# Linear attention beside a mixer MLP, one core: the last tile's queries move ahead of the products with wo, and those products are stacked

## The chip, the core and the metric

The kernel runs on one core of a Trainium2 chip. Five engines work side by side and tell one another by semaphores when data is ready: TensorE (PE in the profile) multiplies, VectorE (DVE) and ScalarE (ACT) do element-wise work, GpSimd (POOL) does the rest of it, and SyncE (SP) issues most DMAs. The metric is the device time of one execution in microseconds, the median of three runs.

## The reference

One sequence of 2048 tokens with 576 features goes through two blocks, and a gate per token mixes the two results:

```
q, k, v = split(x @ wqkv)                  # 32 heads of 18
phi = lambda t: where(t > 0, t + 1, exp(t)) + 1e-6
kv  = einsum("bhsd,bhse->bhde", phi(k), v)   # 18 x 18 per head
z   = sum over tokens of phi(k)
o   = (phi(q) . kv) / (phi(q) . z + 1e-6)
a   = o @ wo
b   = gelu(layernorm(x) @ w1 + b1) @ w2 + b2   # 576 -> 4608 -> 576
out = g * a + (1 - g) * b,   g = sigmoid(sum(x * gate_w))
```

## The kernel before

All products run on rounded operands (`fp32r`): each matrix is split into a high part, rounded, and a low part, the rounding error; a product is the sum of high x high, high x low and low x high. The 576 features are four slices of 128 and a tail of 64, whose high and low parts share one slice. So a projection of 128 tokens on 288 columns (half of 576) takes 14 matmuls: four HH, four HL, four LH and two TAIL, and `BY_ROWS` is the order HH and HL in turn (eight), then TAIL (two), then LH (four).

Every engine keeps program order: the order in which the code calls the operations is the order on each engine, up to the MLP, whose order a planner writes out. All operations go through one helper, so each row of the profile names line 125; they are told apart by their tiles. The stages are:

1. Start. Twelve matmuls on `ones` (`WARM`), then `first_keys` projects the first two tiles of tokens on the first half of the key weights (KEY, 0), with single matmuls on `ones` between the first ones (`warm`) and the transposes of the gate weights (`turn_gate`, into `column`). The second half of the key weights has two columns more, the gate weights and ones, for sums over x; they are written into the raw tile, which is then split as a whole.
2. For each of the 16 tiles of 128 tokens: keys, `phi`, products of x with `phi(k)` summed over all tokens (`add_products`), sums of the keys on GpSimd (`pks`), queries into `acc`. The last three tiles' queries (`late`) are left for stage 3. `jobs` hang other work into this loop by `at(step, ...)`.
3. The kv products: per group of seven heads (`GW` = 126 columns, five groups, the last one shifted so that it is 126 wide too) `wv` times the summed products gives `kv`; `mask_kv` keeps the blocks of one head each. The product of `kv` with `wo` is wanted in slices of 128 rows, so a slice takes pieces of two groups: nine `PIECES`, each with three terms and two halves, 54 matmuls (`project_values`). Each slice's result is taken over by ScalarE (high) and VectorE (low) into `wp`, in two pairs of banks in turn (`w_pairs`).
4. For each tile i: `weigh(i)` (GpSimd, queries times the sums z, into one of three places `qz`), `normalize(i)` (VectorE: reduce, two small operations, the queries in `acc` times the reciprocal), `tail_q(i)`, `transpose_q(i)` (five transposes on TensorE; copies to `qt` on ScalarE, low parts and tail of `qt` on VectorE) and `attend(i)`: 28 matmuls of `qt` with `wp`, per half in the order `BY_ROWS`.
5. The MLP as seven products in place of eight (Strassen), planned ahead, with the mixing at the end. It follows stage 4 and is not touched.

VectorE's two steps for `qt` stand at the end of `transpose_q`, with `q = qt[i]`:

```
dve.tensor_sub(q[:, 5:9], p, raw(q[:, 0:4]))
dve.scalar_tensor_tensor(q[:, 4], raw(q[:, 4]), low_half[:, 0:1], pe_, op0=OP.mult, op1=OP.add)
```

Of the kernel before, what the change touches and what calls it, by code (L numbers as in the profile page):

```python
# [17 lines left out]
P = 128  # L18
S, D, H, DH, F = 2048, 576, 32, 18, 4608
NT = S // P  # L20
# [15 lines left out]
EPS_LN = 1e-5  # L36
WARM = 12
FIRST = 3
# [56 lines left out]
def raw(ap):  # L95
    return ap.bitcast(F32)
# [35 lines left out]
def tile_gated_mix(ctx: ExitStack, tc: tile.TileContext, x, xm, xe, wm, we, wvm, wve, wo, um, ue, w2, b1, b2, gw, out):  # L132
# [95 lines left out]
    def load_w(part, half, pieces=((0, 5),), by=sp):  # L228
        if (part, half) not in wraw:
            wraw[part, half] = wsp.tile([P, 5, HALF + 2], F32, name="s", tag="s")  # L230
        s = wraw[part, half]
        main = wm[part * 2 + half].rearrange("p (t n) -> p t n", t=4)
        tail = we[part * 2 + half]
        for t0, t1 in pieces:
            if t0 < 4:
                by.dma_start(s[:, t0:min(t1, 4), :HALF], main[:, t0:min(t1, 4)])
            if t1 == 5:
                load_twice(s[:, 4, :HALF], tail, by)

    def split_w(part, half, by=dve, pieces=((0, 5),)):  # L240
        w = W[part, half]
        s = wraw[part, half][:, :, :w.shape[2]]
# [46 lines left out]

    def project(i, part, half, order=BY_ROWS, n=None, between={}):  # L290
        w = W[part, half]
        p = banks[i, part, half] = ps[:, next(halves_in) if n is None else n]
        for m, (a, b) in enumerate(order):
            pe.matmul(p[:, :w.shape[2]], xs[i][:, a, :], w[:, b], start=(m == 0), stop=(m == len(order) - 1))
            if m in between:
                between[m]()
# [174 lines left out]


    first = ORDER[:FIRST]
    gwr = spare[0:1, :5 * P]
# [5 lines left out]
    load_x(first[1], True)  # L480
    load_w(KEY, 1)
    load_x(first[2])
# [11 lines left out]
    split_w(KEY, 0, pieces=((0, 1), (1, 2), (2, 4)))  # L494
    split_tail(first[0])
    split_w(KEY, 0, pieces=((4, 5),))

    def first_keys(n, half, between={}):
        project(first[n], KEY, half, WEIGHTS_FIRST if n else HI_FIRST, 3 * half + n, between)
# [19 lines left out]

    first_keys(0, 0, {0: lambda: warm(1), 1: lambda: warm(1), 2: lambda: warm(1), 3: turn_gate})  # L520
    split_x(first[1])
    split_tail(first[1])
    first_keys(1, 0)
    dve.tensor_copy(wraw[KEY, 1][:, :, HALF:HALF + 1], column[:, :, None])
    dve.memset(wraw[KEY, 1][:, :, HALF + 1:HALF + 2], 1.0)
    split_w(KEY, 1, pieces=((0, 2), (2, 4), (4, 5)))
# [45 lines left out]

    PIECES = [(t, j) for t in range(5) for j in (t, t + 1) if j < G]
    kvs = wop_.tile([GW, len(PIECES), P], F32, name="kvs")
    pool.memset(kvs, 0.0)
    ysc = ExitStack()
    ysp = ysc.enter_context(tc.tile_pool(name="ysp", bufs=1, side="right"))
# [6 lines left out]
    def at(n, f, *args):  # L584
        jobs[n].append(lambda: f(*args))

    def load_wo():
        sp.dma_start(wot[:, 0:4], wo[0:4 * GW].rearrange("(t p) n -> p t n", p=GW))
        sp.dma_start(wot[:, 4], wo[D - GW:D])

# [3 lines left out]

    at(3 * 5, sp.dma_start, b1s, b1)
    at(9, load_wv)
    at(40, load_wo)
# [47 lines left out]
    wo_parts = [ym[:GW, a * G * D:(a + 1) * G * D].rearrange("p (j n) -> p j n", j=G) for a in range(2)]  # L645
    kv_parts = [x_places[PLACE[late[0]] % X_RING - 1][:GW], y_place[:GW, :len(PIECES) * P].rearrange("p (t n) -> p t n", n=P)]

    def split_wo(j0, j1):
        hi, lo = (part[:, j0:j1] for part in wo_parts)
        act.activation(hi, wot[:, j0:j1], AF.Copy)  # L650
        dve.tensor_sub(lo, wot[:, j0:j1], raw(hi))

    def mask_kv(n0, n1):
        for n in range(n0, n1):
            t, j = PIECES[n]
            c0 = min(j * GW, D - GW)
            lo, hi = max(j * GW, t * P), min((j + 1) * GW, (t + 1) * P, D)
            own = slice(lo - c0, hi - c0)
            for at_ in (lo - t * P, lo - t * P + 64)[:1 + (t == 4)]:
                dve.tensor_tensor(out=kvs[:, n, at_:at_ + hi - lo], in0=kv[j][:, own], in1=mask[:, own], op=OP.mult)  # L660
        act.activation(kv_parts[0][:, n0:n1], kvs[:, n0:n1], AF.Copy)

    def kv_low(n0, n1):
        dve.tensor_sub(kv_parts[1][:, n0:n1], kvs[:, n0:n1], raw(kv_parts[0][:, n0:n1]))

# [3 lines left out]
    queries_out(late[0])  # L669
    split_wo(4, 5)  # L670
    moments_of(end)
    for part in range(2):
# [59 lines left out]
    project(late[1], QUERY, 1, n=0)  # L732
    kv = [ps[:GW, 1 + j // 3, j % 3 * GW:(j % 3 + 1) * GW] for j in range(G)]
    for j in range(G):
        c0 = min(j * GW, D - GW)
        for t in range(5):
            pe.matmul(kv[j], wv[:, t, c0:c0 + GW], xk[:, t, c0:c0 + GW], start=t == 0, stop=t == 4)
    queries_out(late[1])
    for i in range(1, 3):
        weigh(i)  # L740
    normalize(0, (0,))
    mask_kv(0, 5)
    normalize(0, (1,))
    tail_q(0)
    kv_low(0, 5)
    mask_kv(5, 9)
    kv_low(5, 9)
    w_pairs = cycle((6, 4))

# [14 lines left out]
    def project_values(t):  # L764

        pw = two_of(w_pairs)
        own = [(n, j) for n, (to, j) in enumerate(PIECES) if to == t]
        for half in range(2):
            parts = [(kv_parts[a][:, n], wo_parts[b][:, j]) for a, b in TERMS for n, j in own]
            for m, (a, b) in enumerate(parts):  # L770
                pe.matmul(pw[:, half, :HALF], a, b[:, half_cols(half)], start=m == 0, stop=m == len(parts) - 1)
        p = pw[:, :, :HALF]
        act.activation(halves(wp[:, t]), p, AF.Copy)
        dve.tensor_tensor(out=halves(wp[:, 5 + t]), in0=p, in1=halves(raw(wp[:, t])), op=OP.subtract)
# [17 lines left out]

    project_values(0)
    normalize(1, (0,))
    project_values(1)
    project_values(2)
    project_values(3)
    normalize(1, (1,))
    project_values(4)
    tail_q(1)  # L800
    normalize(2, (0,))
    transpose_q(0)
    normalize(2, (1,))
# [882 lines left out]
```

## Time and profile before

| | |
|---|---|
| median of 3 runs | 1088.93 us (1088.69 to 1089.76) |
| the profiled execution | 1087.51 us, its span 1085.8 us |
| TensorE busy | 1080.8 us |
| VectorE, ScalarE, GpSimd busy | 933.9, 692.7, 242.4 us |
| granted clock of TensorE | 1.000 over the span |

The span goes from the first to the last instruction that the profiler saw; the time of an execution has a little more around it. Busy time of TensorE is modelled, so a share of 100% does not say that every product ran without a gap.

### The profile page before, as it was taken

How to read it: one execution, taken by the hardware profiler on the slowest of the kernel's cores; microseconds unless marked ns; L12 is line 12 of the kernel's file. 1: busy time of each engine (PE TensorE's matmuls, PEld its weight loads, DVE VectorE, ACT ScalarE, POOL GpSimd, SP SyncE). 2: the span in 40 equal slices, each digit the busy share in tenths (PEclk: the TensorE clock that was granted, in tenths of full speed). 3: DMA queues.
4: the chain of work that ended last, by engine and by line, in shares of the span. 5: the costliest groups of instructions: out<-in, count | busy, mean ns of one | idle time of the engine just before them, and what ended most of it. 6: DMA issues, size and time to landing. Idle time of an engine off the chain costs nothing.

```text
span 1085.8 us, 18609 instructions
## 1 busy us (share of the span) xinstructions
PE 1080.8 (100%) x6700; PEld 994.5 (92%) x6700; DVE 933.9 (86%) x1547; ACT 692.7 (64%) x1234; POOL 242.4 (22%) x226
## 2 busy tenths in 40 slices
PE   9999999999999999999999999999999999999998
PEld 9999999999898999998899989998999989999898
DVE  5568787895799999899999998988878888888898
ACT  7677766444668777778887785555545455455642
POOL 2111112431123231322323321121231132112100
PEclk9999999999999999999999999999999999999999
DMA  6356662735744746664656559764544445344432
GB/s 188 126 97 183 177 215 105 311 149 193 246 157 174 248 163 225 202 211 165 205 192 220 180 190 385 244 226 119 158 121 125 119 135 150 119 120 119 142 94 88
DMA packets 116062, 189.65 MB, mean 175 GB/s; under 512 B 8956, under 2 KB 79244, under 8 KB 111874
## 3 DMA queue, kind: packets, MB, share of 16 engines
q1 hardware_dynamic: 115074, 187.72, 53.6%
q8 instruction: 53, 0.87, 0.3%
q10 hardware_dynamic: 704, 0.74, 0.2%
q14 instruction: 39, 0.32, 0.1%
q0 software_dynamic: 192, 0.01, 0.1%
HBM read 121.63 MB, written 66.80 MB: 174 GB/s over the span
## 4 chain that ended last, share of the span: by engine, by line
PE 99%; DVE 0%; ACT 0%; issue 0%
PE ps L125 99%; DVE wp L125 0%; ACT wp L125 0%; DVE ystage L125 0%; DVE ones L125 0%
## 5 line engine op out<-in xcount | busy, mean ns | idle before, releaser
L125 PEld LDWEIGHTS ps<-region,h 128*128 128x128 f32 x3060 | 434.3, 188 | 25.2 <-issue 0.8
L125 PE MATMUL ps<-region,h 128*128 128x288 f32 x3060 | 450.7, 295 | 0.0
L125 DVE TENSOR_TENSOR accs<-ps,accs 128x576 f32<-128x576 f32 x337 | 249.5, 752 | 44.3 <-PE ps L125 37.5
L125 PE MATMUL ps<-y,wa 128*128 128x512 f32 x1008 | 254.9, 392 | 0.0
L125 PEld LDWEIGHTS ps<-y,wa 128*128 128x128 f32 x1008 | 181.9, 188 | 31.8
L125 PE MATMUL ps<-y,wb 128*128 128x512 f32 x756 | 198.6, 393 | 0.0
L125 DVE TENSOR_TENSOR h<-u,h 128x512 fp32r<-128x512 f32 x243 | 170.4, 721 | 7.3 <-ACT u L125 6.8
L125 POOL TENSOR_TENSOR fresh<-fresh 128x288 f32<-128x288 f32 (+1 forms) x99 | 87.5, 886 | 325.4 <-DVE h L125 99.0
L125 PEld LDWEIGHTS ps<-y,wb 128*128 128x128 f32 x756 | 133.8, 188 | 20.7
L125 POOL TENSOR_TENSOR u<-u 128x512 f32<-128x512 f32 x67 | 92.9, 1387 | 245.5 <-ACT u L125 57.9
L125 PE MATMUL ps<-y 128*128 128x288 f32 (+2 forms) x950 | 133.2, 297 | 0.2 <-DVE wp L125 0.2
L125 PEld LDWEIGHTS ps<-y 128*128 128x128 f32 (+1 forms) x950 | 129.7, 188 | 1.8 <-DVE wp L125 0.9
L125 ACT ACTIVATE ps<-ps 128x512 f32<-128x512 f32 (+1 forms) x129 | 79.9, 622 | 72.2 <-PE ps L125 45.0
L125 ACT ACTIVATE region<-fresh 128x576 fp32r<-128x576 f32 (+1 forms) x134 | 82.3, 624 | 62.5 <-PE ps L125 61.5
L125 ACT ACTIVATE u<-ps 128x512 f32<-128x512 f32 x73 | 43.4, 595 | 77.9 <-PE ps L125 76.7
L125 ACT ACTIVATE h<-u 128x512 fp32r<-128x512 f32 x132 | 77.7, 622 | 20.0 <-POOL u L125 10.6
L125 DVE TENSOR_TENSOR region<-fresh,region 128x576 fp32r<-128x576 f32 (+1 forms) x134 | 87.7, 684 | 0.0
L125 DVE TENSOR_TENSOR u<-ps,u 128x512 f32<-128x512 f32 x74 | 50.3, 681 | 15.1 <-PE ps L125 12.8
L125 PE MATMUL ps<-wp,qt 128*128 128x288 f32 x448 | 63.0, 297 | 0.0
L125 ACT ACTIVATE h<-u,b1s 128x512 fp32r<-128x512 f32 x73 | 52.5, 720 | 13.3 <-DVE u L125 12.9
L125 PEld LDWEIGHTS ps<-wp,qt 128*128 128x128 f32 x448 | 59.8, 188 | 0.0
L125 PE MATMUL ps<-ks,xs 128*128 128x448 f32 (+4 forms) x256 | 53.4, 354 | 0.0
(140 smaller groups left out, 1042.2 us busy)
## 6 DMA issues: line engine op xcount, KB each, us to landing
w1d<-wa SPq DMA_DIRECT2D x17, 1280.0 KB
wa<-w1d SPq DMA_DIRECT2D x68, 320.0 KB
fresh<-in_w SPq DMA_DIRECT2D x70, 288.0 KB
y<-yd SPq DMA_DIRECT2D x14, 1280.0 KB
w1d<-wb SPq DMA_DIRECT2D x17, 960.0 KB
wb<-w1d SPq DMA_DIRECT2D x51, 320.0 KB
fresh<-in_um SPq DMA_DIRECT2D x64, 128.0 KB
yd<-ys SPq DMA_DIRECT2D x12, 640.0 KB
```

Of the source, the lines that this page charges most:

```text
L125: self.last = self.tc.keep_in_program_order(op(*args, **kwargs))
```

## The change

It has four parts. At the start, two matmuls on `ones` are dropped and one moved, the second tile's x is split ahead of the key weights' tail, both tiles' TAIL products stand behind their other products, and the two extra columns of the second key half are written straight into the split tile. The products with wo: each of five slices takes its own group of heads (the first 126, the last 72 rows), and the few rows that belong to the next group (2, 4, 6, 8 columns) come as one stacked product: high, low and high rows of `kv` at rows 0, 32 and 64 of `rest_kv`, beside high, high and low rows of `wo` in `rest_wo`, which three pairs of DMAs gather (`gather_rest`). That makes 38 matmuls in place of 54. The operands' unused rows come from casts on GpSimd. The last tile's queries are projected ahead of the products with wo, and `normalize(1)` and `normalize(2)`, the transposes and `queries_out` are placed anew. `w_pairs` has a third pair.

```
-WARM = 12
+WARM = 10
...
-    load_w(KEY, 1)
+    load_w(KEY, 1, ((0, 2), (2, 4), (4, 5)))
...
+    split_x(first[1])
...
+    split_tail(first[1])
...
-    first_keys(0, 0, {0: lambda: warm(1), 1: lambda: warm(1), 2: lambda: warm(1), 3: turn_gate})
-    split_x(first[1])
-    split_tail(first[1])
-    first_keys(1, 0)
-    dve.tensor_copy(wraw[KEY, 1][:, :, HALF:HALF + 1], column[:, :, None])
-    dve.memset(wraw[KEY, 1][:, :, HALF + 1:HALF + 2], 1.0)
+    project(first[0], KEY, 0, HH + LH + HL, 0, {0: lambda: warm(1), 1: lambda: warm(2)}, closes=False)
+    project(first[1], KEY, 0, HH + HL + LH, 1, {7: turn_gate}, closes=False)
+    for n in range(2):
+        project(first[n], KEY, 0, TAIL, n, opens=False)
+    dve.tensor_copy(sums_high[:, :, 0], column)
+    dve.tensor_sub(sums_low[:, :, 0], column, raw(sums_high[:, :, 0]))
...
+    SIZES = [min(GW, D - j * GW) for j in range(G)]
+    kvs = wop_.tile([GW, G, P], F32, name="kvs")
     pool.memset(kvs, 0.0)
+    rest = wop_.tile([DH, G - 1, 8], F32, name="rest")
+    pool.memset(rest, 0.0)
+    rest_wo = wop_.tile([96, G - 2, D], F32R, name="rest_wo")
...
+    kv_place = x_places[PLACE[ORDER[NT - LATE]] % X_RING - 1]
+    rest_kv = kv_place[:96, G:]
+    rest_wo_last = y_place[:96, G * P:G * P + D]
+    at(44, pool.tensor_copy, rest_wo, wot[:96, :G - 2])
+    at(47, pool.tensor_copy, rest_wo_last, wot[:96, G - 2])
+    at(47, pool.tensor_copy, rest_kv, kvs[:96, :G - 1])
...
+    def gather_rest():
+        for at_, part in ((0, 0), (32, 0), (64, 1)):
+            sp.dma_start(raw(rest_wo[at_:at_ + DH]), raw(wo_parts[part][:DH, 1:G - 1]))
+            sp.dma_start(raw(rest_wo_last[at_:at_ + DH]), raw(wo_parts[part][:DH, G - 1]))
...
+    def mask_kv(t):
+        lo, hi = t * P - t * GW, min((t + 1) * P - t * GW, SIZES[t])
+        for at_ in (0, 64)[:1 + (t == 4)]:
+            dve.tensor_tensor(out=kvs[:SIZES[t], t, at_:at_ + hi - lo], in0=kv[t][:, lo:hi], in1=mask[:SIZES[t], lo:hi], op=OP.mult)
+        if t:
+            n = 2 * t
+            dve.tensor_copy(rest[:, t - 1, 8 - n:], kv[t][:DH, :n])
...
+    def kv_high(t0, t1):
+        n = SIZES[t1 - 1]
+        act.activation(kv_parts[0][:n, t0:t1], kvs[:n, t0:t1], AF.Copy)
+        r0, r1 = max(t0 - 1, 0), t1 - 1
+        for at_ in (0, 64):
+            act.activation(rest_kv[at_:at_ + DH, r0:r1, P - 8:], rest[:, r0:r1], AF.Copy)
...
+    def kv_low(t0, t1):
+        n = SIZES[t1 - 1]
+        dve.tensor_sub(kv_parts[1][:n, t0:t1], kvs[:n, t0:t1], raw(kv_parts[0][:n, t0:t1]))
+        r0, r1 = max(t0 - 1, 0), t1 - 1
+        dve.tensor_sub(rest_kv[32:32 + DH, r0:r1, P - 8:], rest[:, r0:r1], raw(rest_kv[:DH, r0:r1, P - 8:]))
...
     split_wo(4, 5)
+    pool.tensor_copy(rest_wo, wot[:96, :G - 2])
+    pool.tensor_copy(rest_wo_last, wot[:96, G - 2])
+    gather_rest()
+    pool.tensor_copy(rest_kv, kvs[:96, :G - 1])
...
-    kv = [ps[:GW, 1 + j // 3, j % 3 * GW:(j % 3 + 1) * GW] for j in range(G)]
...
+    kv = [ps[:n, 1 + j // 3, j % 3 * GW:j % 3 * GW + n] for j, n in enumerate(SIZES)]
...
+    for half in range(2):
+        project(late[2], QUERY, half, n=3 * half)
     normalize(0, (0,))
-    mask_kv(0, 5)
+    for t in range(3):
+        mask_kv(t)
     normalize(0, (1,))
+    mask_kv(3)
+    kv_high(0, 4)
     tail_q(0)
-    kv_low(0, 5)
-    mask_kv(5, 9)
-    kv_low(5, 9)
-    w_pairs = cycle((6, 4))
+    mask_kv(4)
+    kv_low(0, 4)
+    kv_high(4, 5)
+    kv_low(4, 5)
+    w_pairs = cycle((6, 4, 1))
...
-            parts = [(kv_parts[a][:, n], wo_parts[b][:, j]) for a, b in TERMS for n, j in own]
+            parts = [(kv_parts[a][:n, t], wo_parts[b][:n, t]) for a, b in TERMS]
+            if t < 4:
+                parts.append((rest_kv[:, t], rest_wo[:, t] if t < 3 else rest_wo_last))
...
-    project_values(0)
-    normalize(1, (0,))
-    project_values(1)
-    project_values(2)
-    project_values(3)
-    normalize(1, (1,))
-    project_values(4)
+    normalize(1)
     tail_q(1)
-    normalize(2, (0,))
-    transpose_q(0)
-    normalize(2, (1,))
-    for half in range(2):
-        project(late[2], QUERY, half, n=4 + half)
-    transpose_q(1)
+    queries_out(late[2])
+    for t in range(5):
+        project_values(t)
+    normalize(2)
+    for i in range(2):
+        transpose_q(i)
     tail_q(2)
-    queries_out(late[2])
```

TensorE's order at the very start, before the change: `y` are the first projections, `accs` with one column the gate weights' transposes.

```order
L125 MATMUL ps<-ones 128x128 x12
L125 MATMUL ps<-y 128x288
L125 MATMUL ps<-ones 128x128
L125 MATMUL ps<-y 128x288
L125 MATMUL ps<-ones 128x128
L125 MATMUL ps<-y 128x288
L125 MATMUL ps<-ones 128x128
L125 MATMUL ps<-y 128x288
L125 MATMUL ps<-accs 128x1 x5
L125 MATMUL ps<-y 128x288 x24
```

TensorE's order at the same place with the change:

```order
L125 MATMUL ps<-ones 128x128 x10
L125 MATMUL ps<-y 128x288
L125 MATMUL ps<-ones 128x128
L125 MATMUL ps<-y 128x288
L125 MATMUL ps<-ones 128x128 x2
L125 MATMUL ps<-y 128x288 x18
L125 MATMUL ps<-accs 128x1 x5
L125 MATMUL ps<-y 128x288 x8
```

The matmul on `ones` behind the third projection product has moved ahead of it, and the transposes from behind the fourth product to behind the twentieth.

VectorE's order from the second low part of `wp` on, before the change: `den<-qz` opens a `normalize`, `accs<-accs,den` ends it, `qt` are the steps of `transpose_q`.

```order
L125 TENSOR_TENSOR wp<-ps,wp 128x576 x3
L125 SCALAR_TENSOR_TENSOR accs<-accs,den 128x576
L125 TENSOR_TENSOR wp<-ps,wp 128x576
L125 TENSOR_REDUCE den<-qz 128x32
L125 TENSOR_TENSOR den<-den,den_2184 128x32
L125 RECIPROCAL den<-den 128x32
L125 TENSOR_TENSOR qt<-ps,qt 128x512
L125 SCALAR_TENSOR_TENSOR qt<-qt,low_half,ps 128x128
L125 SCALAR_TENSOR_TENSOR accs<-accs,den 128x576
L125 TENSOR_TENSOR qt<-ps,qt 128x512
L125 SCALAR_TENSOR_TENSOR qt<-qt,low_half,ps 128x128
```

VectorE's order from the first low part of `wp` on, with the change:

```order
L125 TENSOR_TENSOR wp<-ps,wp 128x576 x5
L125 TENSOR_REDUCE den<-qz 128x32
L125 TENSOR_TENSOR den<-den,den_2200 128x32
L125 RECIPROCAL den<-den 128x32
L125 SCALAR_TENSOR_TENSOR accs<-accs,den 128x576
L125 TENSOR_TENSOR qt<-ps,qt 128x512
L125 SCALAR_TENSOR_TENSOR qt<-qt,low_half,ps 128x128
L125 TENSOR_TENSOR qt<-ps,qt 128x512
L125 SCALAR_TENSOR_TENSOR qt<-qt,low_half,ps 128x128
```

The end of the third tile's `normalize`, the one with `accs<-accs,den`, has moved ahead of the first tile's two `qt` steps.

GpSimd's order with the change, from the last sums of keys (`pks`) to the first `weigh` (`qz`); before it, the five sums and the five products stand side by side.

```order
L125 TENSOR_TENSOR pks<-pks,k 128x576 x4
L125 CAST rest_wo<-wot 96x1728
L125 TENSOR_TENSOR pks<-pks,k 128x576
L125 CAST y<-wot 96x576
L125 CAST y<-kvs 96x512
L125 CAST rest_wo<-wot 96x1728
L125 CAST y<-wot 96x576
L125 CAST y<-kvs 96x512
L125 TENSOR_TENSOR qz<-accs,pks 128x576 x5
```

Six casts are new, one ahead of the last sum and five behind it.

## Rows read from the trace of the kernel before

**Rows 1.** The page: span, TensorE's share, one group (busy, mean ns).
```profile
span 1085.8 us, 18609 instructions
...
PE 1080.8 (100%) x6700; PEld 994.5 (92%) x6700; DVE 933.9 (86%) x1547; ACT 692.7 (64%) x1234; POOL 242.4 (22%) x226
...
L125 PE MATMUL ps<-y 128*128 128x288 f32 (+2 forms) x950 | 133.2, 297 | 0.2 <-DVE wp L125 0.2
```

**Rows 2.** What TensorE waited for: us in total, times, longest.
```profile
PE ps L125 <- DVE ones L125: 1.1, 1, 1.1
PE ps L125 <- DVE wp L125: 0.2, 1, 0.2
```

**Rows 3.** Time line, TensorE at the start: start us, us, instruction, count.
```profile
6.25 0.41 PE L125 MATMUL ps<-y 128*128 128x288 f32 x1
...
7.33 16.55 PE L125 MATMUL ps<-y 128*128 128x288 f32 x122
```

**Rows 4.** Time line, ScalarE at the start (brackets: idle before, its end).
```profile
5.51 0.68 ACT L125 ACTIVATE y<-s 128x576 fp32r<-128x576 f32 x1 [0.31 <-DMA s<-in_wm]
...
7.55 0.82 ACT L125 ACTIVATE y<-t 128x512 fp32r<-128x512 f32 x2
```

**Rows 5.** Time line, TensorE alone, from the kv products to the first attend.
```profile
183.88 5.66 PE L125 MATMUL ps<-accs,wv 128*126 128x126 f32 x50
189.30 7.99 PE L125 MATMUL ps<-y 126*128 126x288 f32 x54
197.13 0.60 PE L125 MATMUL ps<-accs 128*128 128x128 f32 x4
...
198.03 3.98 PE L125 MATMUL ps<-y 128*128 128x288 f32 x28 [0.19 <-DVE wp L125]
201.84 0.60 PE L125 MATMUL ps<-accs 128*128 128x128 f32 x4
...
202.31 3.95 PE L125 MATMUL ps<-wp,qt 128*128 128x288 f32 x28
```

**Rows 6.** Time line, ScalarE, VectorE and GpSimd, 194 to 209 us.
```profile
194.63 0.65 ACT L125 ACTIVATE wp<-ps 128x576 fp32r<-128x576 f32 x1 [1.14 <-PE ps L125]
195.31 0.76 DVE L125 TENSOR_TENSOR wp<-ps,wp 128x576 fp32r<-128x576 f32 x1 [0.74 <-ACT wp L125]
...
197.89 0.75 DVE L125 SCALAR_TENSOR_TENSOR accs<-accs,den 128x576 f32<-128x576 f32 x1
...
205.40 0.74 DVE L125 TENSOR_REDUCE den<-qz 128x32 f32<-128x576 f32 x1
...
206.22 1.44 POOL L125 TENSOR_TENSOR qz<-accs,pks 128x576 f32<-128x576 f32 x1 [3.24 <-DVE den L125]
...
206.79 1.49 DVE L125 SCALAR_TENSOR_TENSOR accs<-accs,den 128x576 f32<-128x576 f32 x1
...
208.80 0.33 DVE L125 SCALAR_TENSOR_TENSOR qt<-qt,low_half,ps 128x128 fp32r<-128x128 f32 x1
```

**Rows 7.** Time line, GpSimd, VectorE and TensorE around the last sums of keys.
```profile
14.32 0.67 POOL L125 COPY pks<-k 128x576 f32<-128x576 f32 x1 [10.10 <-DVE k L125]
...
169.40 1.43 POOL L125 TENSOR_TENSOR pks<-pks,k 128x576 f32<-128x576 f32 x1 [5.88 <-DVE k L125]
...
170.22 1.23 DVE L125 SCALAR_TENSOR_TENSOR ks<-k,ks 128x576 fp32r<-128x576 f32 x1 [0.96 <-ACT ks L125]
...
172.10 2.62 DVE L125 TENSOR_TENSOR y<-wot,y 126x1152 fp32r<-126x1152 f32 x2
...
176.14 0.46 DVE L125 SCALAR_TENSOR_TENSOR acc<-ps,e 128x288 f32<-128x288 f32 x1 [1.05 <-ACT e L125]
...
177.39 1.88 DVE L125 COPY accs<-ps 128x512 f32<-128x512 f32 x4
...
180.09 3.96 PE L125 MATMUL ps<-y 128*128 128x288 f32 x28
...
181.90 5.72 POOL L125 TENSOR_TENSOR qz<-accs,pks 128x576 f32<-128x576 f32 x4 [11.07 <-ACT pks L125]
```

More of the change, by code (lines that the diff above doesn't have):

```diff
@@ L229, in load_w @@
         if (part, half) not in wraw:
-            wraw[part, half] = wsp.tile([P, 5, HALF + 2], F32, name="s", tag="s")
+            wraw[part, half] = wsp.tile([P, 5, HALF], F32, name="s", tag="s")
         s = wraw[part, half]
@@ L240, in split_w @@
     def split_w(part, half, by=dve, pieces=((0, 5),)):
-        w = W[part, half]
-        s = wraw[part, half][:, :, :w.shape[2]]
+        w, s = W[part, half][:, :, :HALF], wraw[part, half]
         for t0, t1 in pieces:
@@ L288, in tile_gated_mix, with project @@
     halves_in, banks = cycle((6, 7)), {}
-    def project(i, part, half, order=BY_ROWS, n=None, between={}):
+    def project(i, part, half, order=BY_ROWS, n=None, between={}, opens=True, closes=True):
         w = W[part, half]
@@ L293, in project @@
         for m, (a, b) in enumerate(order):
-            pe.matmul(p[:, :w.shape[2]], xs[i][:, a, :], w[:, b], start=(m == 0), stop=(m == len(order) - 1))
+            pe.matmul(p[:, :w.shape[2]], xs[i][:, a, :], w[:, b], start=opens and m == 0, stop=closes and m == len(order) - 1,
+                      skip_group_check=not (opens and closes))
             if m in between:
@@ L470, in load_y @@
         sp.dma_start(raw(Y[:, m]).rearrange("p j s n -> p (j s n)"), yd[sup][:, m].rearrange("p j s n -> p (j s n)"))
+    sums_high, sums_low = W[KEY, 1][:, 0:5, HALF:], W[KEY, 1][:, 5:10, HALF:]
+    dve.tensor_copy(sums_high[:, :, 1], ones[:, :5])
+    dve.tensor_sub(sums_low[:, :, 1], ones[:, :5], ones[:, :5])
     first = ORDER[:FIRST]
@@ L570, in tile_gated_mix @@
     wot = wop_.tile([GW, G, D], F32, name="wot")
-    PIECES = [(t, j) for t in range(5) for j in (t, t + 1) if j < G]
-    kvs = wop_.tile([GW, len(PIECES), P], F32, name="kvs")
+    SIZES = [min(GW, D - j * GW) for j in range(G)]
+    kvs = wop_.tile([GW, G, P], F32, name="kvs")
     pool.memset(kvs, 0.0)
+    rest = wop_.tile([DH, G - 1, 8], F32, name="rest")
+    pool.memset(rest, 0.0)
+    rest_wo = wop_.tile([96, G - 2, D], F32R, name="rest_wo")
     ysc = ExitStack()
@@ L588, in load_wo @@
         sp.dma_start(wot[:, 0:4], wo[0:4 * GW].rearrange("(t p) n -> p t n", p=GW))
-        sp.dma_start(wot[:, 4], wo[D - GW:D])
+        sp.dma_start(wot[:SIZES[4], 4], wo[4 * GW:D])
     def load_wv():
@@ L645, in tile_gated_mix @@
     wo_parts = [ym[:GW, a * G * D:(a + 1) * G * D].rearrange("p (j n) -> p j n", j=G) for a in range(2)]
-    kv_parts = [x_places[PLACE[late[0]] % X_RING - 1][:GW], y_place[:GW, :len(PIECES) * P].rearrange("p (t n) -> p t n", n=P)]
+    kv_parts = [kv_place[:GW, :G], y_place[:GW, :G * P].rearrange("p (t n) -> p t n", n=P)]
     def split_wo(j0, j1):
-        hi, lo = (part[:, j0:j1] for part in wo_parts)
-        act.activation(hi, wot[:, j0:j1], AF.Copy)
-        dve.tensor_sub(lo, wot[:, j0:j1], raw(hi))
@@ L653, in mask_kv @@
[L653 to L661, printed above, removed]
@@ L663, in kv_low @@
-    def kv_low(n0, n1):
-        dve.tensor_sub(kv_parts[1][:, n0:n1], kvs[:, n0:n1], raw(kv_parts[0][:, n0:n1]))
+        n = SIZES[j1 - 1]
+        hi, lo = (part[:n, j0:j1] for part in wo_parts)
+        act.activation(hi, wot[:n, j0:j1], AF.Copy)
+        dve.tensor_sub(lo, wot[:n, j0:j1], raw(hi))
+    def gather_rest():
+        for at_, part in ((0, 0), (32, 0), (64, 1)):
+            sp.dma_start(raw(rest_wo[at_:at_ + DH]), raw(wo_parts[part][:DH, 1:G - 1]))
+            sp.dma_start(raw(rest_wo_last[at_:at_ + DH]), raw(wo_parts[part][:DH, G - 1]))
@@ L732, in tile_gated_mix @@
     project(late[1], QUERY, 1, n=0)
-    kv = [ps[:GW, 1 + j // 3, j % 3 * GW:(j % 3 + 1) * GW] for j in range(G)]
-    for j in range(G):
-        c0 = min(j * GW, D - GW)
+    kv = [ps[:n, 1 + j // 3, j % 3 * GW:j % 3 * GW + n] for j, n in enumerate(SIZES)]
+    for j, n in enumerate(SIZES):
+        own = slice(j * GW, j * GW + n)
         for t in range(5):
-            pe.matmul(kv[j], wv[:, t, c0:c0 + GW], xk[:, t, c0:c0 + GW], start=t == 0, stop=t == 4)
+            pe.matmul(kv[j], wv[:, t, own], xk[:, t, own], start=t == 0, stop=t == 4)
     queries_out(late[1])
@@ L766, in project_values @@
         pw = two_of(w_pairs)
-        own = [(n, j) for n, (to, j) in enumerate(PIECES) if to == t]
+        n = SIZES[t]
         for half in range(2):
-            parts = [(kv_parts[a][:, n], wo_parts[b][:, j]) for a, b in TERMS for n, j in own]
+            parts = [(kv_parts[a][:n, t], wo_parts[b][:n, t]) for a, b in TERMS]
+            if t < 4:
+                parts.append((rest_kv[:, t], rest_wo[:, t] if t < 3 else rest_wo_last))
             for m, (a, b) in enumerate(parts):
```

## The prediction

> **What bounds the kernel now.** I read the page first: TensorE is busy for 1080.8 of 1085.8 us [rows 1]. The reader is to see in this that time can be won in two ways alone: fewer or shorter matmuls, or less waiting of TensorE itself. The list of TensorE's waits names 1.3 us in all [rows 2], but it shows an instruction that stood at its semaphore, not the slack between products, so I read the time line of TensorE at the two places that the change touches. At the start, the third product of the first keys begins at 6.25 because ScalarE's copy of the weight pieces that it needs starts at 5.51 and takes 0.68, behind a DMA [rows 3, 4]. From 7.33 on, 122 products of 288 columns run in 16.55 us, 0.135 us each, and that is the price of a product that waits for nothing [rows 3]. In the middle, the 54 products with wo last from 189.30 to 197.13, that is 0.145 each, and the last tile's queries begin only at 198.03, though the five transposes between (at 197.13) need no more than 0.46, as the next five do from 201.84 to 202.31 [rows 5]. So about 0.55 us lie in gaps between the 54, and some 0.4 ahead of the 28. Everywhere else TensorE is full, so what is won or lost here passes through to the end.
>
> **The sum is made against the profiled execution**, 1087.51 us with a span of 1085.8. The median of the runs shown is 1088.93, 1.42 above it; I add that at the end.
>
> **Start.** Two of the twelve matmuls on `ones` go. The third product still cannot begin before 6.25, so this is worth nothing: the wait for the weight pieces hides it. The matmul on `ones` that stood behind the third product moves ahead of it, into that same wait: two records of 0.11 us (50 records of this kind run in 5.42 us [rows 5]) leave the path, 0.2 us, or 0.35 with the gaps around them. The transposes of the gate weights move into the second tile and cost the same there. The tails' products move behind both tiles; the number of products stays. The new risk is the second tile's x: ScalarE copies it at 7.55 now, behind the weights' tail [rows 4]; the new order lets it go ahead, and TensorE wants it ten products behind the third, at 6.25 + 10 x 0.135 + 0.1 = 7.7. If the copy still began at 7.55 and took 0.6, TensorE would stand for 0.45 us. I take a gain of 0.2, between 0.35 and a loss of 0.25. The loads of the second key half become one issue more on SP's queue and push the later ones back by some 0.6 us; their first use is after 14 us, so I take nothing for it.
>
> **Products with wo.** 54 become 38: 16 x 0.135 = 2.16 us less. Of the kv products the last block is 72 columns wide where it was 126: ten of the fifty records shrink from 0.108 to something between 0.062 (in proportion) and 0.108 (no gain); I take 0.07, near the proportion since the records of before follow one another without a gap, a gain of 0.4. The third pair of banks and the queries ahead of the products take away the gaps, 0.95 us. That would be some 3.5 us together.
>
> **Where it goes.** What was behind those products is now close behind them, and here the order of VectorE decides. Before, it normalises the third tile (`normalize(2)`) in two parts around the first transposes, and TensorE has the 28 products of the last tile's queries to do meanwhile. In the changed order VectorE has, behind the fifth low part of wp, first the whole of `normalize(2)` and only then the low parts of `qt` of the first tile, and TensorE has no more than two sets of transposes (0.46 us each) and eight products to do. The ninth product of `attend(0)` is the pair (4, 4): it reads the tail of `qt`, which VectorE's last of these operations writes.
>
> In times of the profile before: the kv products begin at 183.88 and take 4.3 + 0.7, until 188.9; the queries take 28 products, 3.81 with their restart (198.03 to 201.84), until 192.7; the last of 38 products with wo begins 5.0 later, at 197.7. Its record lasts 0.3 [rows 1], ScalarE's copy 0.65, and VectorE's low part starts 0.68 after the copy does and takes 0.76 [rows 6]: 199.4. The chain that follows stands in the trace of before, for the next tile, in the same order: reduce at 205.40, the two small ones, the normalising, the two low parts of `qt`, the last of which ends at 208.80 + 0.33 = 209.13 [rows 6]. That is 3.73 us, so 203.1, and TensorE hears of it at about 203.2. Before, the ninth product of `attend(0)` stood at 202.31 + 8 x 0.135 = 203.4. Of 3.5 us won, 0.2 are left; the rest is a new wait of about 3 us inside `attend(0)`. The chain holds a collision: the normalising takes 1.49 while GpSimd runs its own product, which the reduce has set free, and 0.75 without [rows 6]. Without it the gain is 0.95. If the short kv records bring nothing, it is 0.2 smaller than taken here or less. I take 0.2, between 0.95 and -0.2. Behind `attend(0)` VectorE has more lead than before (its next reduce starts near 204, behind the two low parts of the second tile's `qt`, and not at 205.40), so I expect no second wait.
>
> **Casts and gathers.** Six casts come to GpSimd: one of 1728 columns ahead of its last sum of keys, five (576, 512, 1728, 576, 512) behind it. The trace has no cast there; its copy of 576 columns takes 0.67 [rows 7], which makes 2.0 and 4.5 us. GpSimd is idle for 11.07 us behind that last sum, until 181.90 [rows 7], so for GpSimd they cost nothing. The six gathers on SP's queue (18 rows each) stand behind the last store and ahead of the loads of w1; their last source is ready at about 177.5, and TensorE wants them at 193.2, so they are hidden by 15 us.
>
> What the casts do to VectorE is the open price. Nearest row: while GpSimd adds keys at 169.40, VectorE's operation at 170.22 takes 1.23, and the normalising doubles in the same company [rows 6, 7]; but GpSimd's part there has two operands. If casts do not hold VectorE up, they cost nothing. If each waits for the other, the 6.5 us of casts meet VectorE's split of wo (172.10, 2.62 us) and what lies around it. VectorE's idle times of 0.96 and 1.05 there [rows 7] absorb 2.0 of it, which leaves a delay of up to 4.5 us, or of 2.5 if only the five later casts count. Its first copy of the sums starts at 177.39 and needs 0.6 of the 1.88 for the four; it frees the bank that TensorE wants at 180.09 [rows 7], a slack of 2.1. So TensorE would lose between 0.4 and 2.4 us; letting the operations take turns one by one I come to 1.9. I take none, since the only rows that show holding-up have two operands on both sides, and keep 1.9 as a case of its own.
>
> The Trainium skill, page "SBUF — State Buffer", section "SBUF: two separate sides", says that VectorE and GpSimd share a port pair as an exclusive lock, and that whichever of an operation on VectorE with two SBUF inputs and one on GpSimd starts first keeps the other out for its whole length. By that rule the casts would block too and the sum would be that of the second case below; the trace agrees for sums (1.49 against 0.75), and no row here shows it for a copy.
>
> **The sum:** 1087.51 - 0.2 - 0.2 = 1087.1; with 1.42, 1088.5, and with restarts of TensorE at the new wait (0.1) 1088.6.
>
> **Rivals.** First, the casts hold VectorE up: 1088.6 + 1.9 = 1090.5. For it speaks the doubling beside GpSimd's sums; against it, that a copy reads one operand only. Second, the new wait does not form, because the tail of `qt` is there when the ninth product wants it: then about 3.2 us come off, and the time is 1087.51 - 0.2 - 3.2 + 1.42 = 1085.5. For it speaks the work removed, which is real; against it, that VectorE takes its instructions in the order shown and has 4.5 us of them from the start of wp's last low part to that tail. Third, on the slower side: casts that run at the pace of GpSimd's sums (1.43 us for 576 columns, [rows 7]) and hold VectorE up. They would last 14 us instead of 6.5 and TensorE would lose up to 9 us, 1097. It decides from a loss of 2.6 us, that is, from casts of 7.2 us in all. Fourth, the gathers land late: slower by over 0.2% only if they land after 195.8, which is 18 us behind their last source; I give it almost nothing.
>
> **How the numbers follow.** A difference under 0.2% (2.2 us) can hardly be told from none by a measurement of this kernel. My forecast (1088.6, no change) has 0.43, the first rival 0.32, the second 0.10, the third 0.12, the rest 0.03. Faster: the second rival and the lucky end of the first case, 0.12. Slower: the third and the upper end of the first rival, 0.14. No change: 0.74. The range leaves out the second rival and most of the third: from 1086.3 (no collision in the chain, 0.75, the full gain at the start and some scatter of the runs) to 1091.3 (upper end of the first rival). The forecast alone would be 1087.6 to 1089.4.
>
> **What would show it.** Right at the start: third product at 6.25 again, and the products with 290 columns about 0.2 us earlier than now. In the middle: 38 products without gaps, then `attend(0)` cut after its eighth product by a wait of 2.5 to 3.3 us for VectorE (`qt`), with `normalize(2)` ahead of it. If that wait is missing or under 1 us, the main step is wrong. If TensorE waits at 178 to 182 for VectorE, with splits of wo longer than 1.3 us beside casts, the first rival holds. Most of the risk lies in the length of the casts, which no row shows, and in the second tile's x.

## The result and the profile after

The changed kernel takes 1091.62 us (median of 9 runs, 1090.31 to 1093.63) beside 1088.93 of the kernel before (9 runs, 1088.31 to 1089.76): a ratio of 1.0027, 95% interval 1.0018 to 1.0036. It is slower, where I had forecast 1088.6 and no change. The nine executions fall into two groups: four with a granted clock of 1.000 over the span take 1090.3 to 1090.9, five with 0.997 or 0.998 take 1091.6 to 1093.6. The profiled execution is the slowest of them, 1093.63 with a span of 1091.5; the one of the kernel before, 1087.51, is faster than all nine of that kernel here, so the 6.1 us between these two profiles are more than the 2.7 between the medians.

The page after: span, TensorE's share and the group of [rows 1].

```profile
span 1091.5 us, 18599 instructions
...
PE 1082.0 (99%) x6680; PEld 995.0 (91%) x6680; DVE 940.4 (86%) x1551; ACT 692.4 (63%) x1238; POOL 250.8 (23%) x233
...
L125 PE MATMUL ps<-y 128*128 128x288 f32 (+2 forms) x928 | 130.6, 297 | 1.7 <-DVE wp L125 1.7
```

TensorE's waits after, where [rows 2] stood:

```profile
PE ps L125 <- DVE qt L125: 2.6, 1, 2.6
PE ps L125 <- DVE wp L125: 1.7, 1, 1.7
PE ps L125 <- DVE ones L125: 1.1, 1, 1.1
PE ps L125 <- DVE accs L125: 0.3, 1, 0.3
```

Two long waits are new, 4.3 us together: the one for `qt` was forecast, the one for `wp` was not. The 0.3 for `accs` stands far behind, at 728 us in the MLP. TensorE's time line shows where the two long ones stand, beside [rows 5]:

```profile
184.50 5.21 PE L125 MATMUL ps<-accs,wv 128*126 128x126 f32 x50
...
195.97 0.56 PE L125 MATMUL ps<-y 126*128 126x288 f32 x3
196.37 0.30 PE L125 MATMUL ps<-rest_wo,y 96*128 96x288 f32 x1
198.32 2.13 PE L125 MATMUL ps<-y 126*128 126x288 f32 x14 [1.66 <-DVE wp L125]
...
201.69 1.32 PE L125 MATMUL ps<-wp,qt 128*128 128x288 f32 x8
205.61 5.17 PE L125 MATMUL ps<-wp,qt 128*128 128x288 f32 x20 [2.60 <-DVE qt L125]
210.57 1.05 PE L125 MATMUL ps<-accs 128*128 128x128 f32 x4
...
211.50 3.72 PE L125 MATMUL ps<-wp,qt 128*128 128x288 f32 x26
```

In the kernel before, `attend(1)` stood here:

```profile
206.56 3.95 PE L125 MATMUL ps<-wp,qt 128*128 128x288 f32 x28
```

The reader is to see three things. The products with `wo` run without gaps until the fourth slice, which needs the first slice's pair of banks again, and there TensorE stands for 1.66 us. `attend(0)` is cut behind its eighth product for 2.60 us. And the 20 products behind that cut take 5.17 us, 0.25 each, where a product costs 0.135 [rows 3]; the four transposes take 1.05 where they took 0.60 [rows 5]. That is the clock. The windows of the same stretch (columns: TensorE's busy time, granted clock, share of the DMA engines, GB/s):

```profile
198.00:202.00 4.00, 3.54 (x26) 1.00 0.23 49
202.00:204.00 2.00, 1.00 (x8) 1.00 1.01 415
204.00:205.00 1.00, 0.00 (x0) 0.86 0.97 410
205.00:206.00 1.00, 0.39 (x1) 0.50 1.04 440
...
208.00:211.00 3.00, 3.00 (x15) 0.50 0.99 415
211.00:212.00 1.00, 1.00 (x8) 0.72 1.04 440
212.00:216.00 4.00, 4.00 (x33) 1.00 1.01 430
```

The granted clock falls from 1.00 to 0.50 (2.4 to 1.2 GHz) while TensorE stands still for `qt`, stays there while it works again, and is back behind 211 us.

So the 5.7 us between the two profiled spans are: 0.6 at the start (the kv products begin at 184.50, before at 183.88), 1.6 more up to the ninth product of `attend(0)`, which begins at 205.61 and not at 203.4, 2.7 for the low clock (`attend(1)` begins at 211.50 and not at 206.56, 4.94 later), 0.5 at 720 to 731 us, where one load for the MLP landed late, and 0.3 that stand at no one place. The chain that ended last shows the late load (start, us):

```profile
720.72 5.53 DMA fresh<-in_w
```

Only one other kept trace, that of the kernel with both moves and the old start below, has such a load in its chain, and whether the change or chance brings it stays open. The wait for `qt` itself adds nothing to this sum: it eats what the shorter work had won.

### The profile page after: what moved, and what is told of

It reads as the page before. It is cut to its first block, busy times and chain, and to the rows that moved or that the text cites. A ratio compares the mean times of both kernels' runs of the same rounds, so it can differ in the third digit from the quotient of the medians.

```text
span 1091.5 us, 18599 instructions
## 1 busy us (share of the span) xinstructions
PE 1082.0 (99%) x6680; PEld 995.0 (91%) x6680; DVE 940.4 (86%) x1551; ACT 692.4 (63%) x1238; POOL 250.8 (23%) x233
## 4 chain that ended last, share of the span: by engine, by line
PE 97%; DVE 1%; DMA 1%; ACT 0%; SPq 0%; issue 0%; ACTq 0%; DVEq 0%
PE ps L125 97%; DMA fresh<-in_w 1%; DVE accs L125 0%; DVE den L125 0%; SPq L125 0%; DVE wp L125 0%; DVE y L125 0%; ACT wp L125 0%; ACT e L125 0%; DVE fresh L125 0%; DVE qt L125 0%; ACT y L125 0%; DVE ystage L125 0%; ACT tail L125 0%; DVE kvs L125 0%
## 5 line engine op out<-in xcount | busy, mean ns | idle before, releaser
L125 PE MATMUL ps<-y 128*128 128x288 f32 (+2 forms) x928 | 130.6, 297 | 1.7 <-DVE wp L125 1.7
L125 PEld LDWEIGHTS ps<-y 128*128 128x128 f32 (+1 forms) x928 | 127.0, 189 | 3.0 <-DVE wp L125 1.9
L125 PE MATMUL ps<-wp,qt 128*128 128x288 f32 x448 | 65.6, 305 | 2.7 <-DVE qt L125 2.6
L125 PEld LDWEIGHTS ps<-wp,qt 128*128 128x128 f32 x448 | 62.1, 194 | 3.2 <-DVE qt L125 2.8
```

The costliest lines, as they stand in the source:

```text
L125: self.last = self.tc.keep_in_program_order(op(*args, **kwargs))
```

## The experiments

**The first tile's transposes ahead of `normalize(2)`.**

```
-    normalize(2)
-    for i in range(2):
-        transpose_q(i)
+    transpose_q(0)
+    normalize(2)
+    transpose_q(1)
```

Expected: 

> The changed kernel with the first tile's transposes and their steps for qt ahead of normalize(2), which then stands between the two sets of transposes. Theory: the 2.6 us wait in attend(0) is VectorE's order alone, and the fall of the granted clock to 0.5 behind it comes from that wait. Then the ninth product of attend(0) starts near 202.8 in place of 205.6, the wait is under 0.5 us, the clock stays at 1.000, the 1.7 us wait for wp in the products with wo stays as it is, and the time is that of the changed kernel's undisturbed executions less 2.6: 1087.8 (ratio to before 0.999). Rival (VectorE has too much work behind the products with wo, whatever its order): the wait moves into attend(1), where normalize(2) and the second tile's qt come late, 1.5 to 2.6 us there, and the time stays at 1090.4 to 1091.6.

Measured: 1088.21 us (11 runs), ratio 1.0001 (0.9992 to 1.0010). TensorE's time line:

```profile
198.72 3.48 PE L125 MATMUL ps<-y 126*128 126x288 f32 x14 [1.66 <-DVE wp L125]
201.99 0.83 PE L125 MATMUL ps<-accs 128*128 128x128 f32 x4
...
203.51 3.98 PE L125 MATMUL ps<-wp,qt 128*128 128x288 f32 x28
...
207.91 3.95 PE L125 MATMUL ps<-wp,qt 128*128 128x288 f32 x28
```

The wait in `attend(0)` is gone and has not moved into `attend(1)`: it was VectorE's order. But the clock was not only that wait's matter. In this execution the 14 products behind the other wait, the one for `wp`, take 3.48 us (2.13 in the changed kernel), at half the clock, as the windows show:

```profile
197.00:199.00 2.00, 0.34 (x3) 1.00 0.00 0
199.00:201.00 2.00, 2.00 (x10) 0.51 0.00 0
201.00:202.00 1.00, 1.00 (x6) 0.50 0.00 0
```

The DMA engines were idle meanwhile, so the heavy DMA traffic beside the low clock in the changed kernel is not needed for the fall. Five of the 11 executions have a clock of 0.998 (1089.0 to 1090.0), six 0.999 or 1.000 (1087.8 to 1088.2).

**`tail_q(1)` behind the second slice of the products with wo.**

```
     normalize(1)
-    tail_q(1)
     queries_out(late[2])
     for t in range(5):
         project_values(t)
+        if t == 1:
+            tail_q(1)
```

Expected: 

> The changed kernel with tail_q(1) behind the second slice of the products with wo; it is ScalarE's only step there that waits for normalize(1). Theory: the 1.7 us wait for wp comes from ScalarE standing at tail_q(1) while the last tile's queries are ready. Then ScalarE's copies of those queries start near 191.9 in place of 195.3, VectorE's first low part of wp at 196.0 in place of 197.5, TensorE waits 0.3 to 0.6 us for wp and the wait in attend(0) stays at 2.5 to 2.9: 1.4 less than the changed kernel, 1090.2, or 1089.0 where the clock does not fall. Rival (VectorE itself, held up by GpSimd's product in normalize(1), is what is late): the low part starts at 197 or later and the time stays at 1090.4 to 1091.6.

To see what this moves, first ScalarE, VectorE and GpSimd in the changed kernel (time line):

```profile
193.00 1.44 POOL L125 TENSOR_TENSOR qz<-accs,pks 128x576 f32<-128x576 f32 x1 [4.77 <-DVE den L125]
...
193.56 1.48 DVE L125 SCALAR_TENSOR_TENSOR accs<-accs,den 128x576 f32<-128x576 f32 x1
195.08 0.31 ACT L125 ACTIVATE tail<-accs 128x128 f32<-128x128 f32 x1 [3.17 <-DVE accs L125]
195.30 0.39 ACT L125 ACTIVATE e<-ps 128x288 f32<-128x288 f32 x1
...
196.85 1.71 ACT L125 ACTIVATE wp<-ps 128x576 fp32r<-128x576 f32 x3
...
197.51 2.08 DVE L125 TENSOR_TENSOR wp<-ps,wp 128x576 fp32r<-128x576 f32 x3
```

ScalarE stands for 3.17 us at the `tail` of the second tile, until VectorE has normalised it at 195.04, and everything that ScalarE has to do for the last tile's queries and for `wp` is queued behind it. VectorE's part takes 1.48 beside GpSimd's product, which began at 193.00: the collision of [rows 6] again. With the move:

```profile
191.59 0.41 ACT L125 ACTIVATE e<-ps 128x288 f32<-128x288 f32 x1
...
194.22 0.65 ACT L125 ACTIVATE wp<-ps 128x576 fp32r<-128x576 f32 x1 [0.18 <-PE ps L125]
...
195.38 1.41 DVE L125 TENSOR_TENSOR wp<-ps,wp 128x576 fp32r<-128x576 f32 x2
```

VectorE's first low part begins at 195.38 in place of 197.51, and the list of waits no longer names `wp`; the ninth product of `attend(0)` begins at 203.47 in place of 205.61, still behind a wait of 2.61:

```profile
203.47 2.93 PE L125 MATMUL ps<-wp,qt 128*128 128x288 f32 x20 [2.61 <-DVE qt L125]
```

The time is 1090.25 us (11 runs), ratio 1.0012 (1.0003 to 1.0021): five executions with a clock of 1.000 take 1088.4 to 1089.1, six with 0.997 or 0.998 take 1090.3 to 1091.1. ScalarE's queue was the cause of the wait for `wp`, and the 2.2 us between the two groups' middles go with the clock. The profiled execution is one of the five; for the six only the mean clock is on record, not the place of the fall.

**Both moves.** Expected: 

> Both orders of the last two kernels together. Theory: both waits go, the clock stays at 1.000, attend(1) begins near 203.8 where it begins at 211.5 in the changed kernel and at 206.6 in the one before; with the later start (+0.6) and no other difference the time is 1088.9 - 2.8 = 1086.1, ratio 0.9975. Rival (VectorE's work is the bound in this stretch): it is no better than the first of the two kernels alone, 1087.8 or more.

Measured: 1086.23 us (11 runs, 1085.43 to 1087.29), ratio 0.9979 (0.9970 to 0.9987). TensorE waits in this stretch for nothing that the list names, the clock is 0.999 or 1.000 in all 11 executions, and the attends follow one another (time line):

```profile
199.86 4.08 PE L125 MATMUL ps<-wp,qt 128*128 128x288 f32 x28
...
204.34 3.96 PE L125 MATMUL ps<-wp,qt 128*128 128x288 f32 x28
```

This beats both kernels with one move alone. VectorE's amount of work in this stretch is not the bound.

**The wait filled.** In the kernel with `tail_q(1)` behind, 18 products more stand in the wait of `attend(0)`:

```
+                if i == 0 and half == 0 and n == 8:
+                    for _ in range(18):
+                        pe.matmul(p[:, 1, :HALF], qt[i][:, 0, :], wp[:, 0, half_cols(1)], start=True, stop=True)
```

Expected: 

> The kernel with tail_q(1) behind (its only long wait is the 2.6 us in attend(0)), and in that wait 18 products more of 288 columns, whose result the second half's first product overwrites. They last 2.4 us, so TensorE has 0.2 us left to wait, and the ninth product begins no sooner or later. Theory: the granted clock falls in some executions because TensorE stood still for 2.6 us there; with the wait filled it stays at 1.000 in every execution, all of them lie with the faster five of the unfilled kernel (1088.4 to 1089.1), and the median falls from 1090.25 to 1088.5 though the kernel does more work. Rival: the clock falls for another reason (the heavier work of this stretch, or chance by execution); then about half of the executions still have 0.997 to 0.998 and the median stays at 1090.2.

Measured: the wait for `qt` is 0.24 us, the ninth product begins at 204.09 (0.6 later than in the unfilled kernel, as the kv products of this execution do already), and the granted clock is 0.999 or 1.000 in all 11 executions.

```profile
204.09 2.93 PE L125 MATMUL ps<-wp,qt 128*128 128x288 f32 x20 [0.24 <-DVE qt L125]
```

The time is 1089.09 us (1088.35 to 1089.46), ratio 1.0001 (0.9992 to 1.0010), against 1090.25: 1.2 us faster with 2.4 us more of useless work. It is 0.6 above my 1088.5. The kernel before, timed beside it, took 0.25 more than beside the unfilled one (1088.84 and 1088.59); the rest is not explained. With the standing still the mean clock was 0.997 or 0.998 in 6 of 11 executions, without it in none of 11, so the fall in this stretch hangs on the standing still; why it comes in about half of the executions and not in all is not shown. Nor need such a wait stand behind every low mean clock: of the 85 timed executions of the kernel before, whose profile lists no wait over 1.1 us, one has 0.998 and took 1092.27. No trace of it is kept.

**The start, in three kernels.** The changed kernel with a raw weight tile two columns wider, as before:

```
-            wraw[part, half] = wsp.tile([P, 5, HALF], F32, name="s", tag="s")
+            wraw[part, half] = wsp.tile([P, 5, HALF + 2], F32, name="s", tag="s")
...
-        w, s = W[part, half][:, :, :HALF], wraw[part, half]
+        w, s = W[part, half][:, :, :HALF], wraw[part, half][:, :, :HALF]
```

the kernel before with the new start alone (the first part of the change, from `WARM` to the extra columns); and the kernel with both moves with that part undone.

Expected of the wider tile: 

> The changed kernel with the raw weight tile two columns wider again, as before, so that the DMAs of the weights write rows of 1152 bytes apart from one another and not two slices in one piece; the computation is the same. Theory: the loads of the key weights in larger pieces on ScalarE's queue are what makes the first tile's x land at 4.9 in place of 3.6 us and the first products start late and at the lower clock. Then x is cast at 3.6, the third product starts near 6.3 in place of 7.1, the products behind it come 0.6 to 0.8 us earlier and the time falls by as much: 1090.9 (1089.8 without the fall of the clock). Rival: the start is later because of the new order of the first copies or by chance of this one execution; then x is cast at the same time as in other runs of the changed order and the time is 1091.6.

Expected of the new start alone: 

> The kernel before with the changed start alone (ten matmuls on ones, second tile's x split early, tails behind both tiles, extra columns written into the split tile); the middle is as before. Theory: the new start loses where I had forecast a gain of 0.2 us. In the five profiles with the new start the first product behind the gate weights' transposes begins at 9.65 to 10.5 in place of about 9.6 by count in the kernel before, and the time around the span is 2.1 us in place of 1.7: 0.5 to 1.0 us slower than before, ratio 1.0005 to 1.001. Rival: the late start of the first profile was chance, and this kernel is 0.2 us faster than the kernel before or equal to it, with 1.7 us around the span.

Expected of both moves with the old start: 

> The kernel with both moves (last tile's stacked products, qt ahead of normalize(2), tail_q(1) behind) and the start of the kernel before. Theory: the start is worth 0.5 to 1.0 us on its own, so this comes to 1085.2 to 1085.7, ratio 0.997, with 1.7 us around the span. Rival: the start is worth nothing either way, 1086.2, or the new one gains its 0.2, 1086.4.

Measured, in this order: 1091.23 us (7 runs, ratio 1.0028, 1.0017 to 1.0039), 1088.87 (11 runs, 1.0000, 0.9991 to 1.0010) and 1086.49 (11 runs, 0.9979, 0.9970 to 0.9988). In time the rivals hold: neither the tile's width nor the start as a whole is worth anything that can be measured. The theory of the first run is half right all the same. VectorE's cast of the first x in it (time line):

```profile
3.79 0.58 DVE L125 CAST y<-t 128x512 fp32r<-128x512 f32 x1 [2.00 <-DMA t<-in_xm]
```

and in the changed kernel:

```profile
4.87 0.43 DVE L125 CAST y<-t 128x512 fp32r<-128x512 f32 x1 [3.12 <-DMA t<-in_xm]
```

With rows apart, x is cast at 3.5 to 3.8 us in all four profiles, with slices in one piece at 4.5 to 5.0 in all nine. But the earlier x brings nothing that can be measured. The piece of the key weights that the third product needs as well is copied by ScalarE at 5.94 in this run and at 5.96 in the changed kernel, and the third product begins at 6.68 here and at 6.34 to 7.09 in the nine with the later x. VectorE's first operation on `kv`, which marks how late TensorE is by then, stands at 187.38, 188.00 and 188.72 in the three profiles with the old start, and between 187.57 and 188.39 in the ten with the new one: the 0.6 us that the changed kernel's profile lost at the start lies within the scatter of single executions.

**Three casts fewer**, in the kernel with both moves.

```
-    at(44, pool.tensor_copy, rest_wo, wot[:96, :G - 2])
-    at(47, pool.tensor_copy, rest_wo_last, wot[:96, G - 2])
-    at(47, pool.tensor_copy, rest_kv, kvs[:96, :G - 1])
```

Expected: 

> The kernel with both moves, without the first set of three casts on GpSimd (the second set writes the same operands, so the result is the same). Theory: the casts hold VectorE up (sums of xs at 164.7 that take 1.1 in place of 0.8 each) but TensorE has slack there, so nothing changes, 1086.2, while VectorE's operations at 164 are short again. Rival: what they hold up reaches TensorE, and 0.5 to 1 us is won.

Measured: 1086.23 us (10 runs), ratio 0.9976 (0.9967 to 0.9985), no different from the run with them (0.9979). What the casts do, in the changed kernel's time line:

```profile
164.07 2.16 POOL L125 CAST rest_wo<-wot 96x1728 fp32r<-96x1728 f32 x1
164.67 2.24 DVE L125 TENSOR_TENSOR xs<-xn,xs 128x512 fp32r<-128x512 f32 x2
...
173.93 1.63 POOL L125 CAST rest_wo<-wot 96x1728 fp32r<-96x1728 f32 x1
173.99 4.52 DVE L125 TENSOR_TENSOR y<-wot,y 126x1152 fp32r<-126x1152 f32 x2
...
179.82 1.87 DVE L125 COPY accs<-ps 128x512 f32<-128x512 f32 x4
```

and in that of the kernel without the first three:

```profile
164.69 0.82 DVE L125 TENSOR_TENSOR xs<-xn,xs 128x512 fp32r<-128x512 f32 x2
```

So 1.4 us of VectorE's 2.24 are the cast's doing, and nothing reaches TensorE: its 28 products of late queries start at 180.72 without these casts and at 180.71 in the changed kernel.

**The time around the span, in two kernels.** It was 1.7 us in the kernel before and 2.1 in the changed one. The first is the kernel with both moves, less one line, the second the kernel before, with casts at the places of the new ones:

```
-    gather_rest()
```

```
+    rest_wo = wop_.tile([96, 2, D], F32R, name="rest_wo")
...
+    at(44, pool.tensor_copy, rest_wo, wot[:96, :2])
+    at(47, pool.tensor_copy, rest_wo[:, 0], wot[:96, G - 2])
+    at(47, pool.tensor_copy, rest_wo[:, 1, :512], wot[:96, G - 2, :512])
...
+    pool.tensor_copy(rest_wo, wot[:96, :2])
+    pool.tensor_copy(rest_wo[:, 0], wot[:96, G - 2])
+    pool.tensor_copy(rest_wo[:, 1, :512], wot[:96, G - 2, :512])
```

Expected of the first: 

> The kernel with both moves, without the six DMAs that gather the rows of wo for the stacked products; these products then multiply the rows that the casts left there, so their part of the result is left out. One look at what lies around the span: 1.7 us in the kernel before and with the new start alone, 2.1 with the new middle, 1.9 with three casts fewer. Theory: it follows the casts on GpSimd, so 2.1 here too. Rival: it follows the six DMAs, so 1.7 here.

Expected of the second: 

> The kernel before with six casts on GpSimd (1152, 576 and 512 columns, twice) at the places of the new ones, into a tile that nothing reads. Theory: the time around the span rises from 1.7 to 2.1 us, VectorE's splits of wo beside the casts take 4 us or more in place of 2.6, and TensorE still waits for nothing there. Rival: the time around the span stays at 1.7; and if the casts' delay reaches TensorE it waits 0.5 us or more between 178 and 182 us.

Measured, one execution each: 1086.14 with a span of 1084.0, so 2.1; and 1088.42 with 1086.4, so 2.0. It follows the casts, not the DMAs: six of them add 0.3 to 0.4 us, and the kernel with three, whose time around the span is 1.9, has 0.2 more. How a cast can cost time outside the span stays open. In the second, VectorE's splits of wo take 3.56 us, less than the 4 expected, and TensorE waits for nothing at 178 to 182.

**The stacked products in the order of before.**

```
-    for half in range(2):
-        project(late[2], QUERY, half, n=3 * half)
...
-    w_pairs = cycle((6, 4, 1))
+    w_pairs = cycle((6, 4))
...
-    normalize(1)
+    project_values(0)
+    normalize(1, (0,))
+    project_values(1)
...
+    normalize(1, (1,))
+    project_values(4)
     tail_q(1)
+    normalize(2, (0,))
+    transpose_q(0)
+    normalize(2, (1,))
+    for half in range(2):
+        project(late[2], QUERY, half, n=4 + half)
+    transpose_q(1)
...
-    for t in range(5):
-        project_values(t)
...
```

Expected: 

> The changed kernel with the stacked products, but the last tile's queries, normalize(1), normalize(2), the transposes and the pairs of banks in the order of the kernel before. Theory: the products with wo come at once behind the kv products, whose low parts are ready only 1.9 us after the last of them (1.2 for the high parts); TensorE waits 1.2 to 1.9 us there, and of the 2.5 us that fewer and narrower products give, with 0.4 more around the span, 0.2 to 0.9 are left: 1088.0 to 1088.7, ratio 0.9992 to 0.9998. Rival: the place of the queries does not matter, and this is as good as the kernel with both moves, 1086.2, ratio 0.998.

Measured: 1089.29 us (11 runs, 1088.98 to 1090.05), ratio 1.0008 (0.9999 to 1.0017), 0.6 above the upper end. Its waits:

```profile
PE ps L125 <- ACT y L125: 1.0, 1, 1.0
PE ps L125 <- DVE wp L125: 0.5, 1, 0.5
PE ps L125 <- DVE y L125: 0.2, 1, 0.2
```

The wait for the high and low parts of `kv` is there, 1.2 us; 0.5 for `wp` stand where two pairs of banks are used again, and in the profiled execution the products from 193 to 196 us ran at a granted clock of 0.50, behind the waits for `kv`. So fewer matmuls alone gain nothing: without the queries in between, TensorE waits for the splitting of the operands behind the kv products. The run undoes the order of the other steps and the third pair of banks as well, and does not tell their shares of the time from one another.

## Why the prediction was wrong

**The new wait in `attend(0)`: right.** I wrote 2.5 to 3.3 us behind the eighth product with `normalize(2)` ahead of it on VectorE; it is 2.60, there, and goes with that order alone. The chain that I took from the next tile holds, collision included (time line of the changed kernel):

```profile
201.85 0.74 DVE L125 TENSOR_REDUCE den<-qz 128x32 f32<-128x576 f32 x1
...
202.67 1.41 POOL L125 TENSOR_TENSOR qz<-accs,pks 128x576 f32<-128x576 f32 x1 [5.17 <-DVE den L125]
...
203.24 1.45 DVE L125 SCALAR_TENSOR_TENSOR accs<-accs,den 128x576 f32<-128x576 f32 x1
...
205.22 0.33 DVE L125 SCALAR_TENSOR_TENSOR qt<-qt,low_half,ps 128x128 fp32r<-128x128 f32 x1
```

The last `qt` step ends at 205.55, 3.70 behind the start of the reduce, for my 3.73. The rival in which it does not form (1085.5) is what the order of both moves gives, 1086.2.

**The step that failed** is "the last of 38 products with wo begins 5.0 later, at 197.7", and with it "38 products without gaps". Behind the late queries I followed VectorE and TensorE, never ScalarE: `tail_q(1)` stood behind all the products with wo before and now stands ahead of them, waits for the end of `normalize(1)`, and holds up the last tile's queries and `wp`. TensorE stood for 1.66 us at the fourth slice, and since the `qt` chain is queued behind `wp` on VectorE, the delay passed through: the last product with `wo` begins at about 200.2 and the ninth of `attend(0)` at 205.61, 2.1 later than with `tail_q(1)` behind. With that one step mended, the ninth product begins at 203.47 for my 203.2, and the executions with a clock of 1.000 take 1088.4 to 1089.1 for my 1088.6. That the time comes out so close is in part luck: the sum lacks the 0.4 us more around the span and counts a gain of 0.2 at the start that did not come, while the kernel before took 1088.59 beside this run and not the 1088.93 that the sum stands on.

**The term that was missing** is the clock. The sum priced a wait of TensorE by its length and 0.1 us of restart. Five of the changed kernel's nine executions have a mean clock of 0.997 or 0.998; in the profiled one of them the matmuls from 205 to 211 us ran at 1.2 GHz. The middle of these five is 2.0 us above that of the others (1092.59 and 1090.55). The missed wait explains 1088.6 to about 1090.5, the clock the rest of the way to 1091.6 in the median and to 1093.6 at worst.

**Smaller terms.** Kv products: 5.01 us from first to last, as forecast (5.0). Start: a gain of 0.2 was forecast, none is measured (1088.87 with the new start alone, 1088.84 for the kernel before beside it). The sign that I named for it, the third product at 6.25 again, did not come either: it begins at 7.08 in the changed kernel, and at 6.25 to 6.59 in the three traces with the old start. Time around the span: 0.4 us more, which I had taken as fixed. Gathers: the list of TensorE's waits names none for them, as forecast.

**The first rival**, casts that hold VectorE up (the "second case" of the paragraph on the skill): half right. They do, though a cast reads one operand only; the six last 1.1 to 2.2 us each, 9.6 in all, more than the 7.2 from which I let the third rival decide. But VectorE's first copy of the sums begins at 179.82, and at 177.39 before [rows 7]: without the 0.62 that this execution was late by already, that is 1.8 us, inside the slack of 2.1, and TensorE lost nothing. The Trainium skill, page "SBUF — State Buffer", section "SBUF: two separate sides", has the shared pair locked by whichever starts first; these rows agree for casts (2.24 us for two operations that take 0.82 alone).

## What to carry to other kernels

When work is moved ahead, follow every engine's queue at the new place, not just the two that exchange the data: a small step that waits for something late (here one copy of 0.31 us) holds up all that is behind it. Then look at what a wait of TensorE drags along: here kernels with a wait of 1.7 to 2.6 us had a lower mean clock in about half of their executions, and in the two such executions that were traced several us of matmuls ran at half the clock, so that even useless products in the wait made the kernel faster. And a gain of fewer matmuls is real only where their operands are ready; here the same 16 matmuls fewer gave 1.0027, 1.0008 or 0.9979, by the order of a few steps and the number of bank pairs.

## What the runs showed of the hardware that was not expected

The granted clock can fall to 0.50 in the middle of a kernel that otherwise holds 1.000, behind a single wait of 1.66 us (the first experiment), and the mean clock is lower in some executions and not in others of the same program (5 of 11 there). With the loads of the weights in rows of 1152 bytes and not in longer pieces, x, which comes on another queue, was cast at 3.5 to 3.8 us and not at 4.5 to 5.0. A cast on GpSimd of one operand holds back VectorE's operations with two (two of them took 2.24 us in place of 0.82). And with six casts on GpSimd the time outside the span that the profiler sees is 0.3 to 0.4 us longer (2.0 to 2.1 in place of 1.7).
